# An S4 convolution with a gated MLP: the residual in four-step pieces, three places for zin, and a new issue order

## The chip, the cores and the metric

One Trainium2 chip, one of its cores. The metric is the device time of one execution in microseconds (us). One launch computes the whole output; the inputs and the output lie in HBM. The kernel uses TensorE (PE), VectorE (DVE) and ScalarE (ACT) for arithmetic, and SyncE (SP) and ACT as the two engines that issue DMAs. GpSimd (POOL) only builds an identity matrix at the start.

## The reference

```python
x = A_u                                  # [1, 2048, 512], float32
xn = layernorm(x)
# S4 branch: a long convolution along the sequence
K = einsum("dn,dnl,dn->dl", C, exp(dt*A*l), dt*B).real      # 2048 taps for each of 512 channels, n = 128 modes
y = irfft(rfft(pad(xn)) * rfft(pad(K)))[:2048] + xn*Dskip
# gate branch: a shifted token mixing, then a channel MLP (512 -> 1376 -> 512)
h  = shift4(gelu(layernorm(xn) @ w1)) @ w2
x1 = xn + h
x1 = x1 + gelu(layernorm(x1) @ w3) @ w4
return x + y * silu(x1)                  # x is the residual of this text
```

## The kernel before

The sequence is cut into 16 steps of 128 rows, one row a partition; `X[:, s]` (128x512) holds step s, and goes through the whole program in place: input, normalised input, `x1`, gate, output. The tap index is factored 32 x 64, so that the transforms are matrix products with constant tables. The 512 channels are worked in two halves (hf 0 and 1) of 256.

The stages, as the program states them: loads and token mixing; `tables(0)` (the taps K of half 0: exponentials and sines on ACT, products of them on DVE, short sums on PE); two of the eight MLP groups; `products(0)`; `tables(1)`; the other six MLP groups; `products(1)`; the gates (`silu` on ACT, one for each pair of steps); the inverse transforms with the multiplication by the gate; the residual; the stores. An MLP group is two steps, in the order `MLP_ORDER = [1,2,3,4,5,6,7,0]`; a label such as mlp7.5 is the last sixth of the last group, group 0.

`products(1)` goes over 8 units. For each it loads a table `cst` (512 KB, from `c_gq`, two places, so that a load waits until the products of two units before have been read), the spectrum inputs `uin` and `kin`, splits them in two half-precision parts (`uh`, `kx`), makes the spectra on PE (`kspec`, `uspec`, in PSUM bank pair pc), multiplies them on DVE (`pr`), transforms back on PE (`inv`, bank pair pd), and stores the result (`z1e`) to scratch in HBM (`scr_Zdb`; half 0: `scr_Zda`). `products(0)` does the same for half 0 in 16 smaller units with `c_gp`.

After a half's products the end of the program reads scratch back: `zin{hf}.{k}` for k = 0 to 7 is one load of 512 KB (`zin`), 16 small matmuls, and two multiplications `X<-X,pd` or `X<-X,pc` of 128x256 on DVE, which need the gate of these steps. The groups go in the order `END_ORDER = [2,3,4,5,6,7,1,0]`. At k = 1, 3, 5 and 7 (half 1: also at 6) `finish{hf}.{k}` adds the residual to four steps (or two) in one DVE instruction and stores them: `out_dram<-X`, one DMA of 128 KB (64 KB for two steps) for each quarter of the partitions. The residual `xr` is x itself, read from HBM a second time.

Every instruction is first recorded by `Plan` and then issued in the order of a table, `ORDER`: the number of an operation, with `a` or `v` where the choice between ACT and DVE is free. So an engine's queue is what the table says, and the line in every row of the profile is that of `issue` (L330). A place in SBUF with a new name waits for the last reader of the old one. DMAs are issued from SP (`Q`) and ACT (`A`); as built, each DMA of the two queues together takes one of eight semaphores in turn, in program order, and is not issued before the DMA eight places ahead of it has landed. An engine that waits to issue a DMA does not go on to its next instruction.

```python
    zinr = [Ring(early, K4, 4), Ring(o, K4, 8)]
    xrs = [early + 4 * K4, o + 13 * K4, late, late + 2 * K4]
```

Here K4 is 4096 bytes a partition. `late` is the place of the `uin` ring of `products(1)` (three places) with the two `cst` places behind it; `o` is that of its other rings. `residual(hf)` loads two pieces of eight steps each, 8192 bytes a partition, as four DMAs of 256 KB; the last of them lies at `late + 2*K4`, half over the `uin` ring and half over a `cst` place.

Of the kernel before, what the change touches and what calls it, by code (L numbers as in the profile page):

```python
# [116 lines left out]
8 19 6 39 3 86 7 1086 2 4 44 0 1 21 5 89 90 87 88 91 92 93 94 95 22 20 10 96 97v 23 9 98a 107 108 102v 105 106  # L117
109 110 111 99a 100 101a 103 104a 145 24 26 25 27 18 35 11 33 112 34 32 113 114 115v 117v 123 124 125 116v 118
168 166 164 170 167 119a 120a 28 30 29 31 142 121 126 122a 169 165 16 13 171 143 127 172 14 173 128 174 46 129
175 176 47 177 144 48 130 146 147 178a 180a 181v 179v 78 148 79a 281 285 283 287 149a 131 152a 153a 204a 185v  # L120
150a 284 132 188 282 288 182v 133 286 134 289 201v 155 189 135 290 15 159 224 291 220 225 136 183 222 221 186
191 192 226 223 190 184a 292 187a 154 227 151 52 228 138a 536 229 537 43 230 293 231 49 366 232 50 294 233 51
194 234 53 193 295 235v 54 199a 236a 198a 368 200 207 297v 140v 210 243v 238v 195a 55 56 205 202 59 208 57 58
141 60 237v 206a 364 538 203a 196a 211 264a 367 239v 137 209 369 213 212 296v 61 217a 218a 197 162 17 247 12 374
240 244 219 365 370 62 241a 304a 245a 260a 214a 248 249 215v 63 246 298v 250 251 67 242 139 68 161 216 45 64 69
300v 253 70 539 257v 268 80 269 65 541 261 375 258a 265 252 270 262v 72 259 271 272 299v 263 371 266a 254a 255a
267 37 81a 274 71 273 163 66 73 278v 74 279v 308 84 321v 256 41 301 305 542 76 40 275v 372 160 276v 309 280 277
302v 380 75 306v 311 312 546 303 544 307 547 325v 77 36 314 313 156 319a 310 570 82 83a 315a 316a 318v 320 332
322 323a 317 373 549 85v 326 333 334 329 540 327v 324 378 548 328 345 346 543 157 550 347 571 551 552 554 553
335 42 339v 572 362 336v 358 330 430 376 337v 340v 338 348 350a 377 382 558 349a 351 341 432 388 545 158 361 433  # L130
555 573 381 575 574 331 383 363 386 452 352a 379 434 423 384 556 454 359 557 427 560 422 559 439 342 576 561 579
577 562 389 343 563a 424 578 390 387 344 428 564 565 566a 385 353a 391 591 438 567a 431 443 592 392 581 593 580
425 569 568 400 594 597 444 435 582 596 583 595 401 455 393 584a 440 429 394 354 612 402 436 395 456 441 403 445
437 396 453 464 613 614 397 585 598 355 615 446 586 404 616 587a 457 399 442 466 458 398 600 419 416 459 417a
426 405 478 480 406 588a 460 599 356 407 360 618 357 479 465 486 408 447a 418 409 461 448 462 617 410 602 463
483 420a 528a 590 449 475 589 421 529a 530 601 532a 533a 641 476a 619 450a 534 472 412 413 620 621 469 633 501
414 603 604 500 473a 634 487 531 535 643 505 451 635 502 644 474 491 751a 646 638 605a 645 730 497 731 494 732
622 733a 847 606 636 477 637 508 623 639 734 640 488 498a 737 738 607 744 499 514 608a 739 495a 609a 745 610
740a 741 624 625 746 647 626a 509a 752a 755a 735 736 411 742 627 648 831 747a 611 743 510 748 753 515a 649 756a
642 496 667 415 652 766 767 650 759 760 749 628 651 757 750 517 511 754 668 761 516 768 769a 773 629a 762a 774  # L140
653 669 670 655 518a 758 780 781 787 788 630a 512a 782 654 763 764 657 656 775a 673 671 513 519 658 659 688 660a
770 676 689 672 776 765 794 771 795 772 832 830 789 801a 690 661 796 783a 777 816 662 691 631 632 663a 664a 665
674 778 809 779 784 790a 802a 692 675 785 786 817 678 810 677 797a 791 693 805a 679 680 697 803 798 694 811 681a
792 806a 709 710 682 711 807 695 793 812a 804 813 823 492 715 818 683 837 799 696 698 712 666 800 814 824 684a
808 713 819a 714 699 825a 1296 1289 1297 826 716 820 1087 717 718 685a 1298 686 687 1088 1290 1291 1310a 700 701
815 821 822 827 720 1095 702a 1292a 703 704 1097 705a 846 1299a 1100 1092 1303 1304 1089 706a 708 707 1098 719
1091 1090 829 1293 467 828 1300 481 1311a 1093 721 722 723a 724 468 1312 863 848 1318 1094 1294 1295 1313 1301
725 1099 1319 1109 1101 1305 1122 1102 1314a 1306a 726a 727a 1307 484 729 1096 1315v 728 1302 1320 1332 1325
1326 1123 470 1308 1309 1321v 1316 1322 485 1106 1124 1103 1105 1104 1317 1107 833 834 493 1108 489 1128 1333
1125 1327 1328a 1323 1324 1329 1111 1110 1127 1346 1347 1339 1340 835 865 1330 1331 849 1334a 866 836a 850 838  # L150
864 482 490 1126 1348 839 471 520 840 841 1112 1113 1114a 1129 1144 842 521 522 1335 1130 862 844a 843a 845 523
1341 1145 1342a 1146 1368 851 853 1369 852a 1336 1349a 1353 1354 1115 854 855 856 857 1131 1343 879 880 1116
# [279 lines left out]
def kernel(  # L432
# [114 lines left out]
    def wavetile(shape, name):  # L547
# [803 lines left out]
```

## Time and profile before

| | |
|---|---|
| three runs | 550.22, 554.72 and 553.86 us, median 553.86 |
| the profiled execution | 549.37 us |
| its span (first to last recorded work) | 547.6 us |
| mean granted TensorE clock | 0.994 of full speed |

The profiled execution is 1.8 us longer than its span, and 4.5 us under the median of the runs. The profile counts as busy the time in which an engine executes arithmetic or loads weights; issuing a DMA and waiting are not counted. "A <- B" behind an idle time says that engine A sat idle until B ended. Rows with `x` and a number stand for as many instructions.

### The profile page before, as it was taken

To read this page: it belongs to the slowest core of one execution; us is meant where nothing else is said; L and a number is where in the kernel's file an instruction comes from. 1 tells how busy PE (TensorE), PEld (TensorE's weight loads), DVE (VectorE), ACT (ScalarE), POOL (GpSimd) and SP (SyncE) were. 2 spreads that over 40 slices of the span, in tenths; PEclk is the share of its full clock that TensorE was granted. 3 is DMA by queue.
4 is the path that set the end of the run, shared out by engine and by line. 5 is a ranking of instruction groups with operands and counts; after the bars stand their busy time and mean duration, and the time that the engine had idled before them with its cause. 6 is when DMAs were issued, how large, how long until landed. Compare 5 with 4: busy or idle time off the path is not lost.

```text
span 547.6 us, 13679 instructions
## 1 busy us (share of the span) xinstructions
PE 520.5 (95%) x5660; PEld 336.6 (61%) x5660; DVE 491.8 (90%) x757; ACT 429.2 (78%) x695; POOL 0.7 (0%) x6
## 2 busy tenths in 40 slices
PE   8999989999999999999999999989999999998983
PEld 8787764544476765666656666655566666766540
DVE  4899999999999999999999899989984999896657
ACT  4799999868999999999889889967766366464630
POOL 0000000000000000000000000000000000000000
PEclk9999999999999999999999999999999999999997
DMA  8986763265847236464376676696689988997996
GB/s 213 208 266 217 232 229 125 85 118 134 135 144 145 41 40 59 60 97 60 117 122 146 135 140 173 139 143 107 134 174 170 297 261 240 294 254 224 311 293 192
DMA packets 210781, 91.40 MB, mean 167 GB/s; under 512 B 155104, under 2 KB 196064, under 8 KB 210336
## 3 DMA queue, kind: packets, MB, share of 16 engines
q1 hardware_dynamic: 206112, 86.08, 66.4%
q10 hardware_dynamic: 4608, 4.46, 2.8%
q8 instruction: 44, 0.72, 0.6%
q14 instruction: 17, 0.14, 0.1%
HBM read 56.96 MB, written 29.36 MB: 158 GB/s over the span
## 4 chain that ended last, share of the span: by engine, by line
PE 45%; DVE 21%; DMA 13%; ACT 12%; SPq 4%; issue 3%; DVEq 0%; ACTq 0%
PE pb L330 15%; PE pa L330 14%; PE pc L330 9%; PE pd L330 7%; DVE wv L330 5%; SPq L330 4%; DVE X L330 4%; ACT mag L330 4%; DMA X<-in_A_u_dram 4%; DMA cst<-c_gq 3%; DVE tm L330 2%; ACT L330 2%; DMA out_dram<-X 2%; DVE pr L330 1%; DMA scr_Zda<-z1e 1%
## 5 line engine op out<-in xcount | busy, mean ns | idle before, releaser
L330 PE MATMUL pb<-x1T,w3h 128*128 128x256 f16 (+1 forms) x1056 | 124.0, 273 | 2.0 <-ACT g L330 1.3
L330 PE MATMUL pa<-w4h,ghl 128*128 128x512 f16 (+1 forms) x528 | 121.9, 379 | 0.0
L330 PEld LDWEIGHTS <-w3h 128*128 128x128 f16 (+1 forms) x1056 | 102.1, 100 | 29.1 <-issue 14.8
L330 PEld LDWEIGHTS <-ghl 128*128 128x128 f16 (+1 forms) x528 | 49.7, 98 | 57.8 <-issue 5.3
L330 ACT ACT_TABLE_LOAD x57 | 73.1, 1283 | 2.6 <-PEq L1339 1.7
L330 ACT ACTIVATE wv<-wv 128x2080 f32<-128x2080 int32 x32 | 62.9, 1964 | 5.5 <-DVE wv L330 5.3
L330 ACT ACTIVATE g<-pb,wsc 128x512 f32<-128x512 f32 (+1 forms) x48 | 31.1, 652 | 10.7 <-PE pb L330 9.8
L330 DVE TENSOR_TENSOR wv<-wv,eg 128x2048 f32<-128x2048 f32 x16 | 36.5, 2283 | 0.0
L330 DVE TENSOR_TENSOR wv<-mag,wv 128x2048 f32<-128x2048 f32 x16 | 36.5, 2281 | 0.0
L330 PE MATMUL pd<-pr,cst 64*128 64x256 f32 x256 | 36.3, 402 | 0.0
L330 DVE SCALAR_TENSOR_TENSOR ghl<-g,wsc,ghl 128x512 f16<-128x512 f32 (+1 forms) x48 | 33.6, 699 | 2.8 <-ACT ghl L330 2.7
L330 PE MATMUL pc<-wv 128*32 128x64 f32 x2048 | 32.6, 220 | 2.4 <-issue 2.4
L330 PEld LDWEIGHTS pc<-wv 128*32 128x32 f32 x2048 | 29.8, 109 | 7.7 <-issue 5.8
L330 ACT ACTIVATE ghl<-g,wsc 128x512 f16<-128x512 f32 (+1 forms) x37 | 25.3, 687 | 10.9 <-PE pa L330 9.9
L330 ACT ACTIVATE mag<-par 128x128 f32<-128x128 f32 x132 | 33.1, 454 | 0.0
L330 ACT COPY z1e<-pd 128x256 f32<-128x256 f32 x51 | 17.2, 376 | 20.2 <-PE pd L330 17.4
L330 ACT ACTIVATE wv<-wv,halfpi 128x2080 f32<-128x2080 f32 x16 | 32.9, 2057 | 0.1
L330 ACT ACTIVATE kh<-pc,ksc 128x256 f32<-128x256 f32 (+1 forms) x37 | 18.2, 541 | 18.6 <-PE pc L330 12.6
L330 PE MATMUL pb<-xT,w 128*128 128x256 f32 x128 | 29.9, 384 | 0.7 <-ACT xT L330 0.7
L330 PEld LDWEIGHTS pd<-pr,cst 64*128 64x128 f32 x256 | 22.2, 186 | 10.9 <-issue 7.5
L330 DVE BATCH_NORM_STATS2 stats<-X 128x6 f32<-128x512 f32 x32 | 21.2, 680 | 7.1 <-DMA X<-in_A_u_dram 7.1
L330 PEld LDWEIGHTS pb<-xT,w 128*128 128x128 f32 x128 | 23.4, 190 | 6.5 <-ACT hT L330 1.1
(167 smaller groups left out, 905.5 us busy)
## 6 DMA issues: line engine op xcount, KB each, us to landing
wst<-in_B_w_dram SPq DMA_DIRECT2D x20, 512.0 KB, 4.4
scr_Ud<-ue SPq DMA_DIRECT2D x16, 512.0 KB, 3.2
scr_Kfa<-k1e SPq DMA_DIRECT2D x16, 256.0 KB, 6.3
uin<-scr_Ud SPq DMA_DIRECT2D x32, 128.0 KB, 2.9
cst<-c_gp SPq DMA_DIRECT2D x16, 256.0 KB, 3.1
kin<-scr_Kfa SPq DMA_DIRECT2D x32, 128.0 KB, 2.7
scr_Zda<-z1e SPq DMA_DIRECT2D x16, 256.0 KB, 3.4
scr_Kfb<-k1e SPq DMA_DIRECT2D x16, 256.0 KB, 5.9
```

Source lines behind the costliest of these rows:

```text
L330: ins = [getattr(self.engines[op.eng], name)(*args, **kw).ins for name, args, kw in op.calls]
```

## The change

The residual comes in pieces of four steps, 4096 bytes a partition: four DMAs of 128 KB each, 32 DMAs in all in place of 16 of 256 KB. Half 0 has two places for its four pieces: pieces 1 and 2 (steps 4 to 7 and 8 to 11) come first, piece 3 takes the place of piece 1 after `finish0.1`, piece 0 that of piece 2 after `finish0.3`. Half 1 has a place for each piece, two in `o` and two at `late`, which no longer reach into a `cst` place. The `zin` ring of half 0 has three places in place of four. `ORDER` is new from the first word to the last: 1984 operations in place of 1968 (the 16 more are the DMAs), and 98 operations change between ACT and DVE.

```diff
 ORDER = """
-8 19 6 39 3 86 7 1086 2 4 44 0 1 21 5 89 90 87 88 91 92 93 94 95 22 20 10 96 97v 23 9 98a 107 108 102v 105 106
...
+3 2 86 0 6 8 5 7 21 20 23 22 9 10 26 87 89 88 90 91 92 24 93 107 1086 105 108 106 25 27 19 94 39 95 96 30 31 11
...
+    class Slots:
+        def __init__(self, *places):
+            self.places = list(places)
+
+        def __call__(self, shape, dt, name):
+            return at(self.places.pop(0), shape, dt, name)
...
-    zinr = [Ring(early, K4, 4), Ring(o, K4, 8)]
-    xrs = [early + 4 * K4, o + 13 * K4, late, late + 2 * K4]
+    zinr = [Ring(early, K4, 3), Ring(o, K4, 8)]
+    xrs = [Ring(early + 3 * K4, K4, 2), Slots(o + 13 * K4, o + 14 * K4, late, late + K4)]
...
-    def residual(hf):
+    def residual(hf, pieces):
         ch = slice(hf * DH, hf * DH + DH)
-        for k in range(2):
+        for k in pieces:
             due(f"xr{hf}.{k}")
-            xr = at(xrs.pop(0), [P, S // 2, DH], F32, "xr")
-            by_r(xr, xv[:, :, k * S // 2 : (k + 1) * S // 2, ch], load=(Q, A))
-            resid.append(xr)
-
-    resid = []
+            xr = xrs[hf]([P, 4, DH], F32, "xr")
+            by_r(xr, xv[:, :, 4 * k : 4 * k + 4, ch], load=(Q, A))
+            resid[hf, k] = xr
+
+    resid = {}
...
     def finish(hf, s0, s1):
         ch = slice(hf * DH, hf * DH + DH)
-        h = S // 2
-        xr = resid[2 * hf + s0 // h]
-        V.tensor_add(X[:, s0:s1, ch], X[:, s0:s1, ch], xr[:, s0 % h : s0 % h + s1 - s0])
+        xr = resid[hf, s0 // 4]
+        V.tensor_add(X[:, s0:s1, ch], X[:, s0:s1, ch], xr[:, s0 % 4 : s0 % 4 + s1 - s0])
         by_r(X[:, s0:s1, ch], ov[:, :, s0:s1, ch], store=(Q, A))
...
-        residual(hf)
+        residual(hf, (1, 2) if hf == 0 else (1, 2, 3, 0))
         for k, g in enumerate(END_ORDER):
...
+            if hf == 0 and k in (1, 3):
+                residual(hf, (3,) if k == 1 else (0,))
```

Three places show what the new order moves. The numbers behind the names tell tiles of one kind apart, and are counted anew in each kernel.

ACT in `products(1)`, from the sixth unit to the seventh. Before (`xr_620` and `xr_630` are pieces of half 0 and half 1; `kh` is the spectrum of the taps, `kx` the split input of the seventh unit, `g32` the gelu of the MLP):

```order
L330 COPY z1e_595<-pd1_99 128x256
L330 COPY z1e_595<-pd0_98 128x256
L330 ACTIVATE kh_606<-pc0_96,ksc_79 128x2x256
L330 ACTIVATE kh_606<-pc0_96,ksc_79 128x256 x2
L330 DMA xr_630<-in_A_u_dram 32x8x256
L330 ACTIVATE kx_614<-kin_612,ksc_79 128x1024
L330 DMA xr_620<-in_A_u_dram 32x8x256
L330 COPY z1e_595<-pd1_99 128x256
L330 ACTIVATE kh_608<-pc0_96,ksc_79 128x2x256
L330 ACTIVATE g32_528<-pb1_95,wsc_76 128x512
```

With the change (`xr_620` and `xr_621` are pieces 1 and 2 of half 0; `xr_632` to `xr_635` are pieces 1, 2, 3 and 0 of half 1):

```order
L331 DMA xr_635<-in_A_u_dram 32x4x256
L331 DMA xr_633<-in_A_u_dram 32x4x256
L331 DMA xr_621<-in_A_u_dram 32x4x256
L331 COPY z1e_595<-pd1_99 128x256
L331 DMA xr_634<-in_A_u_dram 32x4x256
L331 ACTIVATE ghl_527<-g32_526,wsc_76 96x256
L331 DMA xr_621<-in_A_u_dram 32x4x256
L331 ACTIVATE kh_606<-pc0_96,ksc_79 128x256
L331 DMA xr_634<-in_A_u_dram 32x4x256
L331 DMA xr_635<-in_A_u_dram 32x4x256
L331 COPY z1e_595<-pd0_98 128x256
L331 ACTIVATE kx_614<-kin_612,ksc_79 128x1024
```

Before, one issue of a residual load stood ahead of `kx_614` in these rows and one behind it, and three of half 1 came still later; now seven stand ahead of it here, with most of half 1 among them.

ACT at the end of the program, from the last part of the MLP on (`ghl` is the MLP's hidden layer, split in two halves; `ACTIVATE X_89` is a gate). Before:

```order
L330 ACTIVATE ghl_533<-g32_532,wsc_76 128x512
L330 DMA out_0_dram<-X_89 32x4x256
L330 ACTIVATE ghl_535<-g32_534,wsc_76 128x512
L330 ACTIVATE g32_536<-pb1_95,wsc_76 128x512
L330 DMA out_0_dram<-X_89 32x4x256
L330 ACTIVATE ghl_537<-g32_536,wsc_76 128x512
L330 ACTIVATE g32_538<-pb0_94,wsc_76 96x256
L330 DMA out_0_dram<-X_89 32x4x256
L330 ACT_TABLE_LOAD
L330 ACTIVATE X_89<-X_89 128x1024
L330 DMA out_0_dram<-X_89 32x4x256 x2
L330 ACTIVATE X_89<-X_89 128x1024
```

With the change (`xr_624` is piece 3 of half 0, `xr_627` piece 0):

```order
L331 ACTIVATE g32_534<-pb0_94,wsc_76 128x512
L331 DMA xr_627<-in_A_u_dram 32x4x256
L331 DMA out_0_dram<-X_89 32x4x256
L331 ACTIVATE g32_536<-pb1_95,wsc_76 128x512
L331 DMA xr_624<-in_A_u_dram 32x4x256
L331 ACTIVATE g32_538<-pb0_94,wsc_76 96x256
L331 DMA out_0_dram<-X_89 32x4x256 x2
L331 DMA xr_624<-in_A_u_dram 32x4x256
L331 DMA xr_627<-in_A_u_dram 32x4x256
L331 ACT_TABLE_LOAD
L331 ACTIVATE X_89<-X_89 128x1024
L331 DMA out_0_dram<-X_89 32x4x256 x2
```

The `ghl` of the last parts of the MLP are gone from ACT, and four issues of residual loads stand between the stores and ahead of the gate that follows the table load.

DVE around the last MLP sums (`X_89<-pa1_93` and `X_89<-pa0_92` add the MLP's result of group 0 to X). Before:

```order
L330 SCALAR_TENSOR_TENSOR ghl_537<-g32_536,wsc_76,ghl_537 128x512
L330 TENSOR_SCALAR ghl_539<-g32_538,wsc_76 96x256
L330 SCALAR_TENSOR_TENSOR ghl_539<-g32_538,wsc_76,ghl_539 96x256
L330 SCALAR_TENSOR_TENSOR X_89<-pa1_93,wsc_76,X_89 128x512
L330 SCALAR_TENSOR_TENSOR X_89<-pa0_92,wsc_76,X_89 128x512
L330 TENSOR_TENSOR X_89<-X_89,pd1_99 128x256
L330 TENSOR_TENSOR X_89<-X_89,pd0_98 128x256
L330 TENSOR_TENSOR X_89<-X_89,pc1_97 128x256
L330 TENSOR_TENSOR X_89<-X_89,pc0_96 128x256
L330 TENSOR_TENSOR X_89<-X_89,pd0_98 128x256
L330 TENSOR_TENSOR X_89<-X_89,pd1_99 128x256
```

With the change:

```order
L331 TENSOR_SCALAR ghl_539<-g32_538,wsc_76 96x256
L331 TENSOR_TENSOR X_89<-X_89,pd1_99 128x256
L331 SCALAR_TENSOR_TENSOR ghl_539<-g32_538,wsc_76,ghl_539 96x256
L331 TENSOR_TENSOR X_89<-X_89,pc1_97 128x256
L331 TENSOR_TENSOR X_89<-X_89,pc0_96 128x256
L331 TENSOR_TENSOR X_89<-X_89,xr_624 128x4x256
L331 TENSOR_TENSOR X_89<-X_89,pd0_98 128x256
L331 SCALAR_TENSOR_TENSOR X_89<-pa1_93,wsc_76,X_89 128x512
L331 SCALAR_TENSOR_TENSOR X_89<-pa0_92,wsc_76,X_89 128x512
L331 TENSOR_TENSOR X_89<-X_89,pd0_98 128x256
L331 TENSOR_TENSOR X_89<-X_89,pd1_99 128x256
L331 TENSOR_TENSOR X_89<-X_89,pc1_97 128x256
```

Before, the multiplications of the last ten inverses, twenty in all, came behind the two sums. Now four of them are ahead of the sums: two of zin0.6, above the rows shown, and `pd1` and `pd0` of zin1.0. The two of zin0.5 (`pc`, which need the gate of group 7) and the addition of piece 3 have moved down to stand directly ahead of the sums, and sixteen multiplications follow. On PE the same holds: behind the last `pa` matmul stood ten inverses (zin0.6, zin0.7 and all of half 1), and now stand eight, with zin0.6 and zin1.0 moved ahead of it.

## Rows read from the trace of the kernel before

**Rows 1.** The page, part 1: busy time, share of the span, instructions.
```profile
PE 520.5 (95%) x5660; PEld 336.6 (61%) x5660; DVE 491.8 (90%) x757; ACT 429.2 (78%) x695; POOL 0.7 (0%) x6
```

**Rows 2.** Busy time by stretch; columns: window, its length, engines' busy us (instructions), clock, DMA share, GB/s.
```profile
0.00:30.00 30.00, 26.90 (x179) 23.76 (x180) 19.32 (x73) 18.57 (x32) 0.70 (x6) 1.00 0.98 214
30.00:240.00 210.00, 207.39 (x2163) 130.08 (x2162) 205.45 (x310) 198.96 (x337) 0.00 (x0) 1.00 0.56 132
240.00:430.00 190.00, 183.59 (x2233) 117.58 (x2229) 172.93 (x236) 153.14 (x229) 0.00 (x0) 1.00 0.69 139
430.00:503.60 73.60, 69.83 (x710) 48.98 (x708) 66.51 (x90) 44.68 (x83) 0.00 (x0) 1.00 0.93 262
503.60:529.00 25.40, 25.40 (x232) 13.75 (x234) 13.55 (x25) 12.81 (x15) 0.00 (x0) 1.00 0.92 301
529.00:547.60 18.60, 7.42 (x161) 2.48 (x160) 14.04 (x28) 1.06 (x1) 0.00 (x0) 0.81 0.71 211
```

**Rows 3.** What PE waited for: us in total, times, longest.
```profile
PE pd L330 <- DVE X L330: 3.7, 3, 1.8
PE pc L330 <- DMA cst<-c_gq: 2.8, 3, 2.1
PE pc L330 <- issue: 2.4, 1, 2.4
PE pb L330 <- ACT xT L330: 0.7, 1, 0.7
```

**Rows 4.** The chain that ended last, 465 us to the end: start, us, what.
```profile
487.15 7.28 DMA cst<-c_gq
...
521.20 5.09 DMA out_dram<-X
...
526.31 4.20 DMA out_dram<-X
530.51 1.06 ACT X L330
...
537.09 5.94 DVE X L330 x12
...
543.06 0.69 DVE X L330
```

**Rows 5.** DVE's instructions from 529.0 us on, by operation.
```profile
L330 DVE TENSOR_TENSOR X<-X,xr 128x1024 f32<-128x1024 f32 (+1 forms) x6 | 6.2, 1040 | 0.0
L330 DVE TENSOR_TENSOR X<-X,pd 128x256 f32<-128x256 f32 x10 | 3.9, 411 | 0.0
L330 DVE TENSOR_TENSOR X<-X,pc 128x256 f32<-128x256 f32 x10 | 3.7, 414 | 0.6 <-ACT X L330 0.5
L330 DVE SCALAR_TENSOR_TENSOR X<-pa,wsc,X 128x512 f32<-128x512 f32 x2 | 1.4, 746 | 4.3 <-PE pa L330 4.3
```

**Rows 6.** Two inverses on PE in the timeline: start, us, engine, instructions.
```profile
506.08 0.66 PE L330 MATMUL pd<-zin,is 64*32 64x256 f32 x16
506.53 0.64 PE L330 MATMUL pc<-zin,is 64*32 64x256 f32 x16
```

**Rows 7.** The timeline around the end of the MLP; ACTq and SPq are DMA issues.
```profile
521.72 0.72 ACT L330 ACTIVATE ghl<-g,wsc 128x512 f16<-128x512 f32 x1 [1.67 <-PE pa L330]
...
524.37 1.06 ACT L330 ACTIVATE X<-X 128x1024 f32<-128x1024 f32 x1
524.75 4.26 SPq L330 DMA_DIRECT2D out_dram<-X  x2
...
530.51 1.06 ACT L330 ACTIVATE X<-X 128x1024 f32<-128x1024 f32 x1 [5.08 <-DMA out_dram<-X]
```

**Rows 8.** DMA issues of one kind: engine, count, KB each, median us to landing.
```profile
cst<-c_gq SPq DMA_DIRECT2D x8, 512.0 KB, 5.5
...
xr<-in_A_u_dram SPq DMA_DIRECT2D x8, 256.0 KB, 6.2
out_dram<-X SPq DMA_DIRECT2D x14, 128.0 KB, 2.7
```

More of the change, by code (lines that the diff above doesn't have):

```diff
@@ new lines @@
+383 594 431 456 440 595 596 444 400 416 568 392 582 583 401 435 428 612 426 613 393 584a 436 394 441 395 402 437
+453 396 457 465 397 458 445 398 403 459 585 429 442 614 598 447a 417a 418 599 460 569 600 461 404 586 464 478
+479 587a 355 356 615 419 405 449 462 448 617 475 406 463 466 588a 616 532a 486 399 618 407 590 469 357 414 602
+528a 408 533a 641 601 529a 534 621 409 480 603 604 410 476a 619 420a 605a 483 633 620 530 421 535 634 450a 500
+531 502 635 501 505 606 472 638 623 643 644 645 751a 473a 636 477 487 589 451 730 731 607 608a 622 474 637 732
@@ new lines @@
+1349a 1355 869 868a 861 1120 1344 1368 1345 878 897 895 1147 1148 880 1130 1133 1132 1134 1135 870 1136a 871 872
+873 874 1150 1375 876a 894 1356a 1376 1121 1166 1350 875v 877 1149 896 522 1137 523 1167 1360a 883 884a 1168
+1357 1364a 885 886 887 1361a 888 889 913 1369 1365a 898 1138 1362 1151 1152 1366 1351 1169 911 914 890 891a 910
+1352 1363 899 892a 893 901 1367 929 912 1358 1359 930 1170 900a 1171 1377 1139 1370 902 904 903 1140a 905 906
+1378a 907a 908a 1371a 926 1141a 1382 1172 915 909 916a 917 1383 1153 1154 1155 927 928 1372 918 920 1173 919
@@ new lines @@
+1156 1157 1196 1158a 1175 921 1159 1143 1373 943 1188 1189 1389 1384a 1174 1390 1197 1385 1160 922 923a 1192 945
+1177 924a 1161 931 1198 961 1379 946 944 933 932a 959 1199 1142 925 934 1190 1200 1396 1374 1380 1193 936 935
+937 1191 1391 1381 1386 938 1201 1162a 1194 1176 1397 940a 1392a 1163a 1195 1202 1203 942 949 962 1165 960 939a
+947 1410v 1210 1393 1178 1179 1398 948a 950 1403 1404 1418 951 1387 1388 952 1394 953 954 1204 941 1399a 1400
+1223 1180a 1205 1164 1206 1414a 1207 958 1181 1224 977 1411a 956a 955a 957 1405 1419 1182 1208 1229 1395 1406a
@@ new lines @@
+1471a 1472 1047 1073 1279 1280 1596 1626 1049 507 1465v 1281a 1048 1282 1476 1466 1050 1283 1284 1467 1052v
+1051a 1053 1059 1060v 1061 1062 524 1285a 1072 1074 1286a 1459 1473 1581 1064 1063 1065 1070 1483 1066 1496 1474
+1067v 1627 1630v 1288 525 1631 1287 1597 1595 1914 1068a 1598 1069 1628 1477 1478a 1484a 1075 1076v 1913 1077
+1479 1078 1600a 1838 1079 1081 1080 1599 1489 1658 526 1716 1485 1601 1497 1490 1082 1480 1083v 1481 1491 1629
+1582 1656 1659 1686 1583 527 1584 1608 1585 1498 1586 1587 1588 1589 1590 1503 1504 1591 1592 1602v 1505 1603
@@ new lines @@
+1486 1717 1604 1492a 1593 1594 1605a 1625 1632v 1084a 1493 1688 1657 1085 1518 1519 1487 1633 1488 1510v 1687
+1606a 1607a 1614 1615a 1616a 1689 1609 1494 1617a 1511v 1868 1610 1618 1662a 1619 1663 1634 1635a 1636a 1620
+1637a 1611 1613a 1612a 1638 1512 1644 1639 1645v 1660a 1621 1655 1692a 1623v 1499a 1718 1748 1500 1520 1622a
+1640 1693 1525 1646a 1647a 1495 1501 1778 1624 1661 1746 1719 1648 1664 1665a 1666a 1649 1641 1650 1642v 1668
+1667v 1643a 1669 1506v 1514v 1507 1670 1651 1653a 1690a 1674 1678 1675a 1676v 1845 1685 1677a 1691 1679 1747
```

131 lines of the change are left out of this document (53 added, 78 removed), and 7 rows, old and new, of the table ORDER.

## The prediction

> **What bounds the kernel now.** I read the busy times first. PE is busy 520.5 of 547.6 us [rows 1], so at most 27.1 us can go without changing PE's work, and the change leaves PE's instructions as they are. Next comes where those 27.1 us lie [rows 2]: each stretch's length less PE's busy time gives 3.1 us in the first 30 us, 2.6 and 6.4 in the two middle stretches, 3.8 in `products(1)` (430 to 503.6), none from 503.6 to 529.0, and 11.2 after that. In the middle, PE and DVE are both close to full. In `products(1)` the DMA share is 0.93: here PE waits for tables, and the list of what PE waited for names it, 2.8 us in three waits for `cst` [rows 3]. From 503.6 on PE is the bound until 529.0, and then DVE: it is busy 14.0 of the last 18.6 us, and the granted clock of 0.81 in that stretch costs nothing, since PE is done early. The chain of waits shows the end in detail [rows 4]: a load of `cst`, two stores that hold up ACT's gate, and then a run of DVE to 543.75 us (543.06 plus 0.69), 3.9 us before the end of the span, which is the last stores landing. So the residual itself is never on the chain by name. What counts is what its DMAs displace, and what the new order moves.
>
> **The sum is made against the profiled execution,** 549.37 us, of which 547.6 are the span. It lies 4.5 us under the median of the runs, 553.86, and the three runs lie 4.5 us apart (0.8%). A measurement of this kernel can tell about 1% from no change. I take the sum over to the median as it is.
>
> **Head.** The new order issues the loads of X and w1 first and those of the parameters later, and puts two copies of `xT`, which ACT did in a row, on ACT and DVE. PE waits 0.7 us for ACT's `xT` [rows 3]. At most this wait goes; half of it is my value, -0.3 us. The 3.1 us of idle time in this stretch bound the gain; its DMA share of 0.98 [rows 2] bounds the loss at about as much.
>
> **Middle, 30 to 430 us.** Every queue's order is new, with 98 operations changed between ACT and DVE in both directions. PE's idle time is 9.0 us here, 2.4 of them an "issue" gap inside one group of matmuls [rows 2, 3], which no order explains. Any order leaves some waits, and nothing in the rows says that these will be fewer: PE is busy 98.8% and 96.6% of the two stretches. I take 0, with -4 (half of what is idle) and +4 as ends.
>
> **`products(1)`.** There are three effects. First, the pieces lie free of the `cst` places, so half 1's loads need not wait for `cst` to be read, and they are issued earlier, on ACT too. An issue as such is not counted as ACT's work, but ACT waits with what stands behind it: seven loads stand ahead of `kx_614`, the input of the seventh unit, so a load that may not go yet holds up `kx`, then the spectra on PE. Second, the order of the DMAs: by bytes in the issue order, from the fifth unit's `cst` to the last, 6.35 MB go where 7.2 MB went. At 262 GB/s [rows 2] the 0.85 MB are 3.2 us of transfer time, more than the 2.8 us of waits, so these could vanish. Third, between the last two `cst` loads about as much is issued as before (1.4 and 1.5 MB), and it is the last that took 7.28 us to land [rows 4] against a median of 5.5 [rows 8]. The bounds are -2.8 and +3 (one late `kx`, or `cst` as late as the worst). I take 0, since the wait that ends last there sits behind as many bytes as before.
>
> **Tail, PE.** Two inverses move ahead of the last MLP matmul. Two inverses in the timeline end 1.1 us after the first starts (506.08 to 507.17) [rows 6], about 0.52 us each. The stretch to the last `pa` is full on PE [rows 2], so the sums move back by 2 x 0.52 = +1.04 us.
>
> **Tail, DVE.** After the sums, DVE has twenty multiplications at 0.41 us a row, overlapping to 7.6 us by busy time, 0.37 each, and 6.2 us of additions [rows 5]; it works almost without a gap. Four multiplications move ahead of the sums, into the 4.3 us in which DVE waits for PE [rows 5]: 4 x 0.37 = -1.5 us. The additions stay behind as they were: 4096 elements a partition in four instructions of 1024 columns and two of 512. The two multiplications of zin0.5, the addition of piece 3 and one multiplication of zin1.0 now stand right ahead of the sums: 3 x 0.37 + 1.04 = 2.2 us, covered by the same 4.3 us, if their inputs are there.
>
> **Tail, DMA.** Pieces 3 and 0 of half 0, eight DMAs of 128 KB, 1 MB together, can be issued only after `finish0.1` and `finish0.3`, so they go in the stretch from 503.6 to 529 at a DMA share of 0.92 and 301 GB/s [rows 2]: 3.5 us of transfers. Against that, 1 MB of half 1's loads, which were issued at the end of `products(1)`, now go earlier. The stretch has 0.08 x 25.4 = 2.0 us of free DMA time, and the one after it 0.29 x 18.6 = 5.4. I take 0 for the transfers as such. What they can cost is a wait: four of the eight are issued by ACT, ahead of the gate of group 7, and each DMA waits for the one eight places before. The cover can be worked out. The gate ran at 524.37 [rows 7], and the sums start at 529.0 [rows 2], 530.1 with the two inverses. Behind the gate (1.06 us) stand the 2.2 us on DVE, so it must start by 530.1 - 2.2 - 1.06 = 526.8, about 2.4 us later than now. ACT gives away four `ghl` of 0.72 us [rows 7] ahead of it, which offsets the issues themselves, not their waits. So one wait of up to 2.4 us is hidden; a second one isn't.
>
> **Sum:** -0.3 + 0 + 0 + 1.04 - 1.5 + 0 = -0.8 us. That is 548.6 for the profiled execution and **553.1 us** for the median, no change that can be told.
>
> **A rule that speaks against the change.** A residual load of 256 KB landed in 6.2 us, a store of 128 KB in 2.7 [rows 8], so two small ones look no dearer than one large. The Trainium skill, on the page "DMA: Bandwidth & Descriptors", section "Rules for kernel authors", says to coalesce many small transfers into one large one, and its section "Anatomy of one DMA — SWDGE (gpsimd) path" gives each DMA a fixed cost of about 2.0 us besides its bytes; sixteen more DMAs would by that rule be dearer where DMAs queue. What it would do here is the third rival.
>
> **Rivals.** *The late pieces block ACT (slower).* In the profile a store issue at 526.31 held ACT's queue 4.20 us until 530.51, behind another store of 5.09 us [rows 4], and SP's issue of two stores took 4.26 us [rows 7]. ACT then sat idle 5.08 us ahead of its last gate [rows 7]. With four loads more in the queue, ahead of an earlier gate that is needed sooner, the same can happen twice: 5.09 + 4.20 = 9.3 us, less the 2.4 of cover, is +6.9, or 560.0 us. It decides from the point where the two waits together pass 2.4 us; one wait of 4.2 us alone gives +1.8, 554.9, and is in the forecast's case. Against it: in the chain only these two waits of the kind stand after the products, and the gate of group 7 had none. *The freed places take the waits away (faster).* The waits for `cst` (2.8) and the "issue" gap (2.4) go [rows 3], and with them half of the other 6.6 us in the middle (3.3): 553.1 - 8.5 = 544.6 us. The 0.85 MB speak for the first; for the rest there is only that the order is new. Without the middle's share it is 547.9. *Small DMAs are dear (slower, hardly to be told).* If a piece of 128 KB took the 6.2 us of a large one, the eight late loads would hold the DMA queues 8 x 3.1 = 24.8 us longer; eight are in flight at most, so 3.1 us: 556.2. The 2.7 us of a store of that size speak against it. *The change does nothing of what it says:* only three of the 32 loads come before `products(1)` in the new order, and if DVE's tail waits for its loads instead of the sums, the 1.5 us don't come: 554.6, within the forecast's case.
>
> **How the numbers follow.** The forecast, no change to be told (548.3 to 559.4), has 0.54, with the fourth rival and the one-wait form of the first in it; faster by the freed places 0.24; the blocked ACT 0.18; dear small DMAs 0.04, of which nearly all lies within 1%. The chances: faster 0.24, same 0.57, slower 0.19. The likeliest case's own range is 548.3 to 557. For 8 in 10 the range reaches to 545.5, near the full form of the second rival, and to 560, the full form of the first.
>
> **What would show it.** In the profile after, PE's wait for `cst` at 2 to 4 us and PE idle 7 to 11 us from 30 to 430 would show the middle terms right. The two inverses show in the last `pa` ending about 1 us later against the last `pd<-pr`, and the four multiplications as DVE's run after the sums about 1.5 us shorter. The cover is right if the two sums follow the last `pa` at once. I would be wrong, slower, if the sums wait for `xr`, or for the gate with a DMA named ahead of it; and faster, if `cst` leaves the list of waits and PE's idle time in the middle falls under 5 us.

## The result, and the profile after

| | before | changed |
|---|---|---|
| median | 548.38 us (20 runs, 545.59 to 554.72) | 551.48 us (20 runs, 547.99 to 553.47) |
| profiled execution | 549.37 us | 552.34 us |
| its span | 547.6 us | 550.6 us |
| mean granted clock | 0.994 | 0.983 |

The ratio of the changed kernel to the one before is 1.005, with a 95% interval of 1.0031 to 1.0069. Run again later (the run changed_again below) it was 1.0086 (1.0058 to 1.0115). So the change makes the kernel slower, by about 2.7 us in the first comparison and 4.7 in the second. I had forecast 0.8 us less. The forecast's 553.1 us is near 551.48 only because its base, the median of three runs, lay 5.5 us above the median of twenty; what counts is the difference, and its sign was wrong.

The two profiled executions differ by 2.97 us. The page of the changed kernel, first part (engine, busy us, share of the span, instructions; compare [rows 1]):

```profile
PE 524.0 (95%) x5660; PEld 337.1 (61%) x5660; DVE 493.0 (90%) x763; ACT 427.3 (78%) x689; POOL 0.7 (0%) x6
```

PE has the same instructions and is busy 3.5 us longer, which no instruction count explains; the mean clock of 0.983 hints at why. The stretches (stretch, length, busy us of PE, weight load, DVE, ACT and POOL, granted clock, DMA share, GB/s) answer to [rows 2]:

```profile
30.00:240.00 210.00, 207.62 (x2182) 131.32 (x2181) 206.78 (x317) 202.08 (x343) 0.00 (x0) 1.00 0.59 133
240.00:430.00 190.00, 184.68 (x2243) 117.49 (x2242) 173.43 (x237) 151.34 (x226) 0.00 (x0) 1.00 0.70 140
430.00:503.60 73.60, 70.12 (x690) 47.35 (x691) 64.53 (x88) 44.10 (x82) 0.00 (x0) 0.98 0.83 243
```

In `products(1)` the DMA share fell from 0.93 to 0.83. What PE waited for (tile, releaser, us in all, times, longest), against [rows 3]:

```profile
PE pc L331 <- DVE kh L331: 2.8, 1, 2.8
PE pd L331 <- DVE X L331: 2.7, 2, 1.9
PE pc L331 <- DVE X L331: 2.6, 3, 1.1
...
PE pd L331 <- DMA zin<-scr_Zda: 0.7, 1, 0.7
...
PE pc L331 <- DMA cst<-c_gq: 0.5, 1, 0.5
```

The waits for `cst` fell from 2.8 us to 0.5, as the best case of the prediction had it. In their place stands one new wait of the same size, for `kh`, the spectrum of the taps. The chain of waits (start, us, what) shows where it comes from:

```profile
482.84 5.42 DMA cst<-c_gq
488.27 0.02 issue
488.29 0.32 ACTq L331
...
488.71 0.70 ACT kh L331
...
489.43 0.48 DVE kh L331
489.91 0.39 DVE ghl L331
490.30 0.41 DVE kh L331
...
490.84 1.08 PE pc L331 x12
```

The timeline of ACT over the same time (start, us, what; in brackets the idle time before it and what ended it):

```profile
483.23 1.15 ACT L331 ACTIVATE kx<-kin,ksc 128x1024 f16<-128x1024 f32 x1
488.29 0.32 ACTq L331 DMA_DIRECT2D xr<-in_A_u_dram  x1
488.71 0.69 ACT L331 ACTIVATE kh<-pc,ksc 128x512 f32<-128x512 f32 x1 [4.32 <-DMA cst<-c_gq]
```

ACT finished `kx` at 484.38 and next had to issue one DMA of `xr_620`, piece 1 of half 0. In the order of the built program (not in that of `ORDER`'s words, where it is the second DMA behind) that DMA stands eight places behind the last `cst` load, so it takes the same semaphore and could go only when that load had landed, at 488.27. Behind the issue in ACT's queue stood `kh_608`, whose input PE had finished by 485.6. DVE needs `kh` to release bank pair pc, and PE needs the bank:

```profile
482.71 1.48 PE L331 MATMUL pb<-x1T,w3h 128*128 128x256 f16 x12
484.12 0.85 PE L331 MATMUL pc<-kx,cst 128*64 128x256 f16 x12
484.80 0.82 PE L331 MATMUL pc<-uh,cst 128*64 128x256 f16 x12
...
490.84 1.08 PE L331 MATMUL pc<-kx,cst 128*64 128x256 f16 x12 [2.75 <-DVE kh L331]
491.85 2.74 PE L331 MATMUL pb<-x1T,w3h 128*128 128x256 f16 x12
494.52 0.92 PE L331 MATMUL pc<-uh,cst 128*64 128x256 f16 x12
```

PE stood still for 2.75 us, and then ran slower: twelve matmuls of `pb` took 2.74 us, where the same twelve took 1.48 at 482.71. The stretches behind the wait say why (last columns: granted clock, DMA share, GB/s):

```profile
491.00:492.00 1.00, 1.00 (x13) 0.59 (x10) 1.00 (x1) 0.04 (x1) 0.00 (x0) 0.66 1.08 303
492.00:494.00 2.00, 2.00 (x11) 1.40 (x10) 1.34 (x4) 0.65 (x1) 0.00 (x0) 0.50 0.66 254
494.00:495.00 1.00, 1.00 (x11) 0.56 (x11) 0.15 (x1) 0.37 (x1) 0.00 (x0) 0.64 0.01 3
495.00:497.00 2.00, 2.00 (x30) 1.52 (x24) 1.47 (x2) 1.12 (x3) 0.00 (x0) 1.00 0.00 0
```

The granted clock was 0.50, the 1.2 GHz level, from 492 to 494, behind the idle time, and was full again from 495 on. The Trainium skill, page "TensorE: Matmul & The Clock Gate", section "HAM oscillation — how this bites in real kernels", describes this: a wait for a transfer that leaves PE idle drops the clock, and the group behind it starts slow. The rows agree: 0.50 behind 2.75 us of idle time, though here PE waits for the transfer by way of ACT and DVE.

Not every such wait did this. In the kernel before, PE's longest wait for `cst`, 2.08 us at the same place of `products(1)`, left the granted clock at 1.00, and the same twelve matmuls of `pb` took 1.48 us behind it (two rows of the timeline and one of the stretches):

```profile
494.48 0.85 PE L330 MATMUL pc<-kx,cst 128*64 128x256 f16 x12 [2.08 <-DMA cst<-c_gq]
...
495.91 1.48 PE L330 MATMUL pb<-x1T,w3h 128*128 128x256 f16 x12
...
495.00:496.00 1.00, 1.00 (x19) 0.80 (x16) 0.63 (x1) 0.55 (x1) 0.00 (x0) 1.00 1.12 222
```

So the new wait cost more than its own length, and the old one did not.

Cut at four moments, the two executions differ like this (us; the moments are the first `pc<-kx` matmul of `products(1)`, the end of the last `pa`, the end of DVE's last addition and the end of the span):

| | before | changed | difference |
|---|---|---|---|
| up to the first `pc<-kx` | 430.78 | 429.15 | -1.63 |
| from there to the last `pa` | 98.25 | 102.07 | +3.82 |
| to DVE's end | 14.72 | 14.05 | -0.67 |
| to the end of the span | 3.84 | 5.28 | +1.44 |
| together | 547.59 | 550.55 | +2.96 |

The second row is one stretch of each trace. Kernel before:

```profile
430.78:529.03 98.25, 94.48 (x932) 62.08 (x936) 79.32 (x113) 56.91 (x98) 0.00 (x0) 1.00 0.92 272
```

Changed kernel:

```profile
429.15:531.22 102.07, 97.84 (x961) 62.62 (x967) 80.71 (x119) 54.99 (x93) 0.00 (x0) 0.98 0.85 253
```

PE's idle time is 3.77 us before and 4.23 after. Its busy time is 3.36 us longer: the two inverses that moved ahead of the last `pa`, and the slow clock.

The last row of the table is the stores. DVE's last addition in the changed kernel, and the issues behind it (SPq and ACTq are issues, drawn from the first to the last of a run):

```profile
544.58 0.69 DVE L331 TENSOR_TENSOR X<-X,xr 128x512 f32<-128x512 f32 x1
...
545.27 1.47 ACTq L331 DMA_DIRECT2D out_dram<-X  x3
545.29 2.04 SPq L331 DMA_DIRECT2D out_dram<-X  x4
```

DVE ends at 545.27, but SP issues stores until 547.3. In the kernel before DVE ended at 543.75, and two stores were left for each engine:

```profile
543.78 0.79 SPq L330 DMA_DIRECT2D out_dram<-X  x2
543.78 0.86 ACTq L330 DMA_DIRECT2D out_dram<-X  x2
```

The new order left stores of earlier additions to the end of the queues, some of them on SP behind stores that wait for a later addition.

### The profile page after: what moved, and what is told of

Its sections match the earlier page's. It is cut to its first block, busy times and chain, and to the rows that moved or that the text cites. A ratio compares the mean times of both kernels' runs of the same rounds, so it can differ in the third digit from the quotient of the medians.

```text
span 550.6 us, 13718 instructions
## 1 busy us (share of the span) xinstructions
PE 524.0 (95%) x5660; PEld 337.1 (61%) x5660; DVE 493.0 (90%) x763; ACT 427.3 (78%) x689; POOL 0.7 (0%) x6
## 4 chain that ended last, share of the span: by engine, by line
PE 63%; ACT 17%; DMA 10%; DVE 7%; issue 3%; ACTq 0%; SPq 0%; DVEq 0%
PE pb L331 25%; PE pa L331 18%; PE pc L331 10%; PE pd L331 10%; ACT mag L331 4%; ACT L331 3%; DMA X<-in_A_u_dram 3%; ACT wv L331 2%; DVE wv L331 2%; DMA cst<-c_gq 2%; DVE X L331 2%; DMA scr_Kfb<-k1e 2%; DMA zin<-scr_Zda 1%; DMA x1T<-x1h 1%; ACT EB L331 1%
## 5 line engine op out<-in xcount | busy, mean ns | idle before, releaser
L331 PE MATMUL pb<-x1T,w3h 128*128 128x256 f16 (+1 forms) x1056 | 125.6, 275 | 0.7 <-ACT g L331 0.7
L331 PE MATMUL pa<-w4h,ghl 128*128 128x512 f16 (+1 forms) x528 | 123.4, 380 | 0.0
L331 PE MATMUL pb<-w,hT 128*128 128x512 f32 x58 | 26.4, 596 | 0.5 <-ACT hT L331 0.5
L331 PE MATMUL pa<-w,hT 128*128 128x512 f32 x58 | 26.5, 598 | 0.0
```

What stands on the lines that cost most here:

```text
L331: ins = [getattr(self.engines[op.eng], name)(*args, **kw).ins for name, args, kw in op.calls]
```

## The experiments

There are ten runs, of nine new kernels and of the changed kernel again. The common table uses the stretches from above (us, one profiled execution each). The time up to the first `pc<-kx` is left out: it goes from 426.9 to 430.8 over these kernels, and it differs by 3.9 us between the kernel before and `old_order_small`, which has the old order. The ratios are each against the kernel before as it ran beside them, with its interval; the stretches are of a single execution.

| kernel | ratio to before (95%) | first `kx` to last `pa` | to DVE's end | to the end | sum |
|---|---|---|---|---|---|
| before | 1 | 98.25 | 14.72 | 3.84 | 116.81 |
| changed | 1.005 (1.0031 to 1.0069) | 102.07 | 14.05 | 5.28 | 121.40 |
| changed_again | 1.0086 (1.0058 to 1.0115) | 101.97 | 14.04 | 5.12 | 121.13 |
| late_issue | 1.0009 (0.998 to 1.0038) | 98.06 | 13.76 | 5.17 | 116.99 |
| sp_piece | 0.9989 (0.9963 to 1.0016) | 97.84 | 13.84 | 5.07 | 116.75 |
| four_zin | 1.0098 (1.0061 to 1.0135) | 105.05 | 14.04 | 5.21 | 124.30 |
| early_stores | 1.007 (1.0039 to 1.01) | 102.25 | 14.05 | 4.88 | 121.18 |
| old_order_small | 0.9977 (0.9946 to 1.0009) | 96.88 | 14.72 | 4.10 | 115.70 |
| late_sorted | 1.0031 (1.0003 to 1.0058) | 98.51 | 17.80 | 3.31 | 119.62 |
| late_tail | 0.9974 (0.9943 to 1.0004) | 96.00 | 15.11 | 3.49 | 114.60 |
| tail_only | 1.006 (1.0029 to 1.0091) | 100.59 | 16.50 | 3.56 | 120.65 |
| sp_tail | 0.9979 (0.995 to 1.0008) | 98.33 | 15.11 | 3.51 | 116.95 |

**late_issue** moves one word of the order, ACT's issue of `xr_620`, past `kh` (numbers are words of `ORDER`):

```diff
-1772a 1790 1812a 1846 1539 1813 1925
+1772a 1790 1812a 1539 1813 1925
...
-1535 1774 1538 1843 1821
+1535 1774 1538 1843 1846 1821
```

> The changed kernel with one word of the order moved: ACT's issue of the first piece of half 0 (xr_620) stands behind the last table-fed products instead of ahead of kh_608. Theory A, a wait for a turn: in the changed kernel this issue waited from 484.4 to 488.29 us for the cst load eight DMAs ahead to land, held up kh_608 on ACT, and PE idled 2.75 us and then ran a group of 12 matmuls in 2.67 us instead of 1.42 at a lower granted clock. Then PE's wait for kh goes to under 0.5 us (what is left of the landing of cst at about 488.3), the clock stays at 1.00 up to 529 us, and the time falls by 3.0 to 4.0 us: 547.5 to 548.5 against 551.5, ratio to the kernel before 0.998 to 1.000. Rival B, the tail's DMAs set the end: what PE gains is lost to landing loads and stores behind 503 us, and the time falls by less than 1 us, ratio 1.003 to 1.006.

Measured: 547.14 us, ratio 1.0009. ACT does `kh` as soon as PE has made its input:

```profile
484.00 0.69 ACT L330 ACTIVATE kh<-pc,ksc 128x512 f32<-128x512 f32 x1 [0.63 <-PE pc L330]
```

The wait for `kh` is gone from PE's list, the clock is full throughout `products(1)`, and the stretch from the first `kx` to the last `pa` is 4.01 us shorter than in the changed kernel:

```profile
427.46:525.52 98.06, 96.33 (x961) 62.03 (x967) 81.00 (x119) 55.09 (x93) 0.00 (x0) 1.00 0.89 263
```

With the same instructions PE is idle 1.73 us instead of 4.23 (2.50 less), and busy 1.51 us less at the full clock. So the one misplaced issue cost 2.5 us of waiting and 1.5 us of slow clock.

**four_zin** gives half 0 its fourth `zin` place back, in the changed kernel:

```diff
-    zinr = [Ring(early, K4, 3), Ring(o, K4, 8)]
-    xrs = [Ring(early + 3 * K4, K4, 2), Slots(o + 13 * K4, o + 14 * K4, late, late + K4)]
+    zinr = [Ring(early, K4, 4), Ring(o, K4, 8)]
+    xrs = [Ring(early + 4 * K4, K4, 2), Slots(o + 13 * K4, o + 14 * K4, late, late + K4)]
```

> The changed kernel with four places for half 0's zin instead of three, the residual's two places moved up by one, and the order untouched. In the changed kernel the load of zin0.6 was issued at 512.31 us, right after the third inverse before it had read its place, landed after 7.54 us, and PE waited 0.75 us for it. Theory A: the three places cost no more than that wait, the time falls by 0.3 to 1.0 us, ratio to before 1.003 to 1.005. Rival B, the tail's DMAs set the end: with the fourth place the zin loads go earlier, the loads of pieces 3 and 0 behind them on SP too, and the time falls by 1.5 us or more, ratio under 1.003.

Measured: 552.34 us, ratio 1.0098, so no better than the changed kernel. The wait for `zin`, 0.75 us in the changed kernel, grew:

```profile
521.55 0.67 PE L331 MATMUL pd<-zin,is 64*32 64x256 f32 x16 [1.77 <-DMA zin<-scr_Zda]
```

The load of zin0.6 is issued at 511.97, about as in the changed kernel (512.31), since its place in SP's queue decides and not the ring; it landed after 9.45 us, 7.54 in the changed kernel. The wait for `kh` (2.9 us) stayed, and the clock stayed low for longer behind it. None of my theories expected a longer stretch. Whether this kernel is slower than the changed one the intervals leave open (1.0098 against 1.005 and 1.0086); giving the place back, in this order, gained nothing.

**early_stores** moves three left-over stores, one of `finish0.1` and two of `finish0.3`, ahead in SP's and ACT's queues, right behind the load of zin1.1:

```diff
+1931 1860 1877 1880 1576v
-1931 1576v
...
-1908 1880 1907
+1908 1907
...
-1910 1860 1937
+1910 1937
...
-1960 1877 1959
+1960 1959
```

> The changed kernel with three stores of half 0 (one of finish0.1, two of finish0.3), which the order issues at 536.3, 536.7 and 542.5 us though their data are ready by 514, moved up behind the load of zin1.1, that is to about 526. In the changed kernel the last store is issued at 547.02 us, 1.75 after DVE's end at 545.27; in the kernel before it was 0.45 after. Theory C, SP's queue of stores is too full at the end: the last issue follows DVE's end by 0.5 to 0.9 us and the time falls by 0.8 to 1.3 us, ratio to before 1.0025 to 1.0037. Rival: the stores' landing itself takes longer there (2.47 us against 2.39 speaks against it), the time stays within 0.4 us of the changed kernel's.

Measured: 551.03 us, ratio 1.007. The time from DVE's end to the end of the span is 4.88 us instead of 5.28, so 0.4 of the 1.44 came back: the last issue still goes 1.43 us after DVE's end, since stores of half 1's earlier additions stand on SP behind those of the last one. The count of left-over stores mattered less than their order.

**old_order_small** is the kernel before with the small pieces alone, at the old places and in the old order, each load word doubled:

```diff
-    xrs = [early + 4 * K4, o + 13 * K4, late, late + 2 * K4]
+    xrs = [early + 4 * K4, early + 5 * K4, o + 13 * K4, o + 14 * K4, late, late + K4, late + 2 * K4, late + 3 * K4]
...
-            xr = at(xrs.pop(0), [P, S // 2, DH], F32, "xr")
+            xr = at(xrs.pop(0), [P, 4, DH], F32, "xr")
```

> The kernel before with its own order and places, and each residual load of 256 KB split in two of 128 KB, issued one behind the other on the same engine: 32 small DMAs and nothing else of the change. If small DMAs are dear in themselves (the prediction's third rival) it is slower than before by 2 to 4 us, ratio 1.004 to 1.007, in the landing of the loads. If only bytes count, it stays within 1 us, ratio 0.998 to 1.002. A third way: the sixteen more DMAs shift whose landing each issue waits for, and a new wait of 1 us or more shows at one place, with the others as before.

Measured: 545.02 us, ratio 0.9977; sixteen more DMAs cost nothing that can be told. DMA issues (count, size, median us from issue to landing; 256 KB took 6.2 on SP, [rows 8]):

```profile
xr<-in_A_u_dram SPq DMA_DIRECT2D x16, 128.0 KB, 5.5
xr<-in_A_u_dram ACTq DMA_DIRECT2D x16, 128.0 KB, 5.0
```

A piece of half the size lands only 0.7 us sooner on SP, but these loads have time to spare, and the kernel pays nothing for it. So the loss does not sit in the size of the pieces. In this trace PE does not wait for `cst` at all, though its last piece still lies over a `cst` place. The rule to coalesce, which the prediction took from the Trainium skill (page "DMA: Bandwidth & Descriptors", section "Rules for kernel authors"), fits the landing times and is not borne out by the kernel's time. (The 2.0 us that the prediction set beside it are, as the title of their section says, for DMAs of the GpSimd path; these loads are issued by SP and ACT.)

**sp_piece** leaves `ORDER` alone and issues all four DMAs of that one piece from SP, whose queue does no arithmetic:

```diff
-            by_r(xr, xv[:, :, 4 * k : 4 * k + 4, ch], load=(Q, A))
+            by_r(xr, xv[:, :, 4 * k : 4 * k + 4, ch], load=(Q,) if (hf, k) == (0, 1) else (Q, A))
```

> The changed kernel with its order untouched, but piece 1 of half 0 (xr_620) issued by SP alone instead of SP and ACT. The turn that falls behind the last cst load then belongs to another load on SP (xr_632), so the wait for the landing of cst is still there, on the other engine. Theory A (what costs is ACT's queue behind the waiting issue, not the load, its bytes or the late landing): PE's wait for kh is under 0.5 us, no fall of the clock, the stretch from the first kx matmul to the last product is 70 to 71 us as with the issue moved (69.9; 73.1 in the changed kernel), ratio to before 0.998 to 1.003. Rival: the turn costs wherever it stands, since SP then holds back the store of z1e and the zin loads; PE waits as long elsewhere, ratio 1.004 to 1.007.

Measured: 547.0 us, ratio 0.9989. The turn eight places behind the last `cst` load now falls to another load, `xr_632`, and on SP, where it waits until that load has landed; no arithmetic stands behind it. From the list of what SP waited for:

```profile
SPq L331 <- DMA cst<-c_gq: 3.4, 1, 3.4
```

PE waits for no `kh`, and the timeline shows the groups close together at full speed:

```profile
488.30 0.85 PE L331 MATMUL pc<-kx,cst 128*64 128x256 f16 x12 [0.43 <-ACT z1e L331]
489.08 1.48 PE L331 MATMUL pb<-x1T,w3h 128*128 128x256 f16 x12
```

The stretch up to the last `pa` is 4.23 us shorter than in the changed kernel, and 4.13 shorter than in changed_again: two kernels without the wait on ACT, and the same size of gain.

**late_sorted** is late_issue with early_stores' move, and with the four stores of each later `finish` directly behind its addition; one slice of the table:

```diff
-1906 1954
+1906 1907 1908 1909 1910 1954
...
-1935 1968
+1935 1936 1937 1938 1939 1968
```

> The kernel with the late issue (ratio 1.0009), and the stores of the tail put in the order in which their additions end: the three left-over stores of half 0 behind the load of zin1.1, and the four of each later finish directly behind it. With only the three moved, stores of earlier finishes still stood on SP behind one that waited for the last addition, and the last issue followed DVE's end by 1.43 us. Theory C, the queues' order at the end: the last issue follows DVE's end by 0.4 to 0.9 us as in the kernel before (0.45), the span ends 3.8 to 4.3 us after DVE's end (5.2 with the late issue alone), ratio 0.998 to 0.9995. Rival: the end of the stores is set by their landing under load, and the span still ends 4.8 us or more after DVE's end, ratio 1.000 to 1.002.

Measured: 549.46 us, ratio 1.0031. DVE's end to the end of the span went down to 3.31 us, from 5.17 in late_issue. DVE ended some 4 us later here, which by itself gives the earlier stores time; but late_tail, tail_only and sp_tail, with the same order of stores and without that delay, have 3.49 to 3.56. So the order of the stores was the cause of the +1.44. SP now held the load of zin1.7 back behind stores (issued 534.65, landed 541.73), and PE waited for it:

```profile
541.87 1.11 PE L330 MATMUL pc<-zin,is 64*32 64x256 f32 x16 [4.69 <-DMA zin<-scr_Zdb]
```

**late_tail** is late_sorted with the load of zin1.7 ahead of the stores, and the inverses of zin0.6 and zin1.0 back behind the last `pa`, where all ten then alternate between the two bank pairs as in the kernel before; slices of it:

```diff
-1557 1899 1558
+1557 1558
...
-1579 1842
+1579 1899 1903 1842
...
-1957 1894
+1957 1975 1894
```

> The one with late issue and sorted stores, and the two inverses zin0.6 and zin1.0 put back behind the last MLP matmul with their four multiplications, all ten inverses then alternating between the two bank pairs as in the kernel before. By the prediction's terms this costs +0.46 us (PE 1.04 sooner, DVE 1.5 more behind it). By the changed kernel's trace moving them had cost 1.2 us on PE and given only 0.7 behind it, since DVE sat idle there in gaps, so putting them back gives 0.3 to 0.7 us. The first: last pa to DVE's end 15.0 us or more against 13.8, ratio 0.0008 above that of the sorted stores; the second: 14.3 to 14.7 us, the last pa 1.0 to 1.3 us sooner after the last product, ratio 0.0005 to 0.001 below.

Measured: 546.1 us, ratio 0.9974. With as many inverses ahead of the last `pa` as in the kernel before, PE is idle 1.20 us in place of 3.77:

```profile
428.71:524.71 96.00, 94.80 (x929) 61.71 (x935) 79.42 (x115) 55.10 (x93) 0.00 (x0) 1.00 0.88 262
```

Against late_issue PE is busy 1.53 us less up to the last `pa`: that is the price of the two inverses. Behind it DVE needs 1.35 us more (15.11 for 13.76). Moving them is a wash, as far as one execution of each can tell.

**tail_only, sp_tail, changed_again** ran on one chip: the changed kernel with late_tail's tail, sp_piece with that tail, and the changed kernel itself. Slices of the common tail:

```diff
-1557 1899 1558
+1557 1558
...
-1579 1842
+1579 1899 1903 1842
...
-1906 1954 1932
+1906 1907 1908 1909 1910 1932
```

> The changed kernel with the tail of the late_tail run alone (two inverses back behind the last MLP matmul, stores in the order of their additions, the load of zin1.7 ahead of them), and ACT's issue of xr_620 left where the change put it, waiting for the last cst load. If the two losses add, PE still waits 2.5 to 3.0 us for kh and runs at half the clock behind it, the span ends 3.3 to 3.9 us after DVE's end, and the ratio to before is 1.000 to 1.003 (the changed kernel's 1.005 less the 0.0035 that the tail gave). If one hides the other, it stays at 1.004 or more.

> Both repairs without moving the issue: piece 1 of half 0 issued by SP alone, and the tail of the late_tail run. If the losses add, PE's wait for kh and the fall of the clock are gone, the stretch from the first kx matmul to the last product is 69 to 71 us, the span ends 3.3 to 3.9 us after DVE's end, and the ratio to before is 0.994 to 0.998: clear of the kernel before. If a new wait takes their place (a zin load behind stores, as with the sorted stores alone), it is 0.999 or more.

> The changed kernel itself, unaltered, on the chip of the two repairs. The wait for kh (2.75 us) and the granted clock of 0.50 behind it were in its first profile; if they belong to the order and not to that execution, they show again (2.5 to 3.2 us, 0.50 for 3 us or more) and the ratio is 1.003 to 1.007.

Measured: 550.13, 545.76 and 550.77 us, ratios 1.006, 0.9979 and 1.0086. tail_only is late_tail with a single word of `ORDER` at its old place, ACT's issue of `xr_620`: 1.006 against 0.9974, and 4.59 us more up to the last `pa`. The wait for `kh` is there in tail_only (2.4 us) and in the second run of the changed kernel, and so is the low clock behind it; in sp_tail neither is. The changed kernel, second run:

```profile
PE pc L331 <- DVE kh L331: 2.5, 1, 2.5
```

tail_only and sp_tail differ in who issues that one piece, and by 4.4 us, 0.8%. Up to the last `pa` they differ by 2.26 us only, since sp_tail waited for `cst` instead:

```profile
PE pc L330 <- DMA cst<-c_gq: 2.7, 2, 1.4
```

The tail alone gives about 0.6 us (550.77 to 550.13), within what the intervals leave open, though it mends 1.6 us of the stores. One reason shows in tail_only: ACT's last gate came late, which had not happened in late_tail:

```profile
530.74 0.91 ACTq L330 DMA_DIRECT2D out_dram<-X  x2
531.70 1.06 ACT L330 ACTIVATE X<-X 128x1024 f32<-128x1024 f32 x1 [5.06 <-DMA xr<-in_A_u_dram]
```

DVE waited 1.85 us for it there, 0.46 in late_tail (16.50 us from the last `pa` to DVE's end against 15.11).

No mended version is clear of the kernel before by its own interval. late_issue, sp_piece, late_tail and sp_tail, with 0.9974 to 1.0009, all lie under the changed kernel's 1.0031 to 1.0069, three of them with their whole interval; late_issue's ends at 1.0038.

## Why the prediction was wrong

**The step that failed** is `products(1)`: "I take 0, since the wait that ends last there sits behind as many bytes as before." Up to the last `pa` the changed kernel lost 3.82 us, of which the two inverses are 1.53; what is left for this term is +2.3. My reason for 0 did not hold: the wait that ended last there was no longer the one for `cst`, and that load itself landed after 5.42 us in place of 7.28. Both ends that I had set showed in the trace, and I let them cancel. The `cst` waits went from 2.8 us to 0.5: in late_issue, where no wait for `kh` replaces them, PE is idle 2.04 us less than before over the whole stretch (1.73 for 3.77). And the load "that may not go yet" held ACT, though not where I looked: I counted seven loads ahead of `kx_614`, and the harm came one instruction further, at `kh_608`. The wait was to be found without a run: the order of the built program says which DMA stands eight places ahead of an ACT issue, and here it was the last `cst` load, whose 7.28 us to landing stand in the chain [rows 4] and in my working.

**The clock had no term.** I priced a late `kx` at up to 3 us of waiting. The wait measured 2.50 us net, and the matmuls behind it another 1.51 at the 1.2 GHz level: 4.0 us for one issue, above my bound of +3. I had read the low clock only at the program's end, where it costs nothing.

**The rival of the blocked ACT** had the mechanism right, an ACT issue waiting for its turn ahead of work that PE needs, but I put it into the tail only, at 560.0 us and with 0.18. In the changed kernel's tail it did not happen: the last gate started 0.04 us after the sums. In tail_only it did, once, for 1.4 us.

**Tail, PE** (+1.04) measured +1.53 by PE's busy time, half as much again: the pair in the timeline [rows 6] runs back to back (and gives 1.09 us for two, so 0.55 each, not 0.52), while the two that moved stand alone among other matmuls.

**Tail, DVE** (-1.5) gave -0.67. The multiplications did move. The price of 0.37 each (0.38 by the rows: 7.6 us for twenty) holds for instructions that do not wait for each other. The kernel before, timeline of DVE:

```profile
533.83 0.42 DVE L330 TENSOR_TENSOR X<-X,pd 128x256 f32<-128x256 f32 x1
534.16 1.22 DVE L330 TENSOR_TENSOR X<-X,xr 128x1024 f32<-128x1024 f32 x1
```

The addition starts 0.09 us before the multiplication ahead of it ends. In the changed kernel most additions stand right behind their own multiplications:

```profile
541.77 0.75 DVE L331 TENSOR_TENSOR X<-X,pc 128x256 f32<-128x256 f32 x2
542.56 1.22 DVE L331 TENSOR_TENSOR X<-X,xr 128x1024 f32<-128x1024 f32 x1
543.79 0.75 DVE L331 TENSOR_TENSOR X<-X,pc 128x256 f32<-128x256 f32 x2
```

Here it starts 0.04 us after the end. That is 0.12 us or so at each of four more places, 0.5 us; the other 0.3 are gaps ahead of multiplications that wait for PE, such as 0.11 us ahead of 538.38, where an overlap could stand. This is read from the traces; no run tried it. The additions behind the sums are 5120 elements a partition, not 4096, by the forms that the prediction lists itself; no term hung on it.

**Tail, DMA** (0): the transfers were covered, but I weighed only what ACT issues ahead of the gate, not the order of the stores behind it, which is +1.44. late_sorted and the three runs with its order of stores show that it was this order.

**Head and middle** (-0.3 and 0): the 0.7 us wait for `xT` stayed, and PE's idle time in the middle is 7.7 us (2.38 and 5.32), within the 7 to 11 that I had named. The 1.63 us by which the changed kernel is ahead at the first `kx` are less than the scatter between profiled executions, so neither term can be told from 0.

**Small DMAs** cost no time (old_order_small). That the freed places took the `cst` waits away is not shown: with the old places these waits were 2.8 us in one execution and absent in another (old_order_small), with the freed places 0.5 to 2.7 (sp_tail). So of the 2.96 us between the two executions one issue (4.0), the two inverses (1.53) and the order of the stores (1.44) are more than the whole; the shorter waits elsewhere in the stretch (2.04), DVE's part (0.67) and the time ahead of `products(1)`, which scatters, pay back the rest.

What stays open: what sets the waits for `cst`; whether the new order, mended, is better than the old one (late_tail and sp_tail at 0.9974 and 0.9979 do not exclude 1), and the new order with pieces of eight steps, which was not tried, because its places do not hold them.

## What to carry to other kernels

Where DMAs take a fixed number of semaphores in turn, look up for every issue on an engine that also computes which DMA stands that many places ahead of it, and when that one lands; if it is a large load in a loaded stretch, what stands behind the issue is late by that much. Move such an issue behind the work that others wait for, or to an engine that only issues. Look at the clock behind a wait of TensorE before you price it: here 2.5 us of waiting cost 4.0, while the 2.08 us of the kernel before cost no more than themselves.

## What the runs showed of the hardware

- Behind PE's idle time of 2.75 us the granted clock was 0.50, and a group of twelve matmuls took 2.74 us for 1.48. The low clock came back in all five profiles with the wait for `kh` (2.44 to 2.96 us). Behind the 2.08 us in the kernel before it stayed at 1.00. No run varied the length of a wait by itself.
- Loads of one size landed after very different times: 512 KB of `zin` after 7.54 us in the changed kernel and 9.45 in four_zin, issued at 512.31 and 511.97 us, and 512 KB of `cst` after 5.42 (7.28 in the kernel before). No run tried what sets it.
- At the end of the program, an addition on DVE starts 0.07 to 0.09 us before the end of a multiplication whose result it does not need, and 0.04 us after the end of one whose result it does.
